# Making the first pairs' sums and stages between the last filter groups, and loading x and v ahead of the spectra

## The chip, the core and the metric

The kernel runs on one core of one Trainium2 chip. The metric is the time of one execution on the device in microseconds. The engines are TensorE (PE, with its weight loads as PEld), VectorE (DVE), ScalarE (ACT), GpSimd (POOL) and SyncE (SP), whose queue issues almost all DMAs. Each engine works through its own instructions in the order in which the program issues them.

## The reference

A long convolution is followed by two MLP blocks. With x and v of shape (2, 12480, 128):

```python
h_filt = (np.maximum(pos_emb @ w1, 0.0) @ w2) * np.exp(-0.01 * pos)[:, None]
u = x * v
L = 2 * S
Uf = np.fft.rfft(u, n=L, axis=1)
Hf = np.fft.rfft(h_filt, n=L, axis=0)
y = np.fft.irfft(Uf * Hf[None], n=L, axis=1)[:, :S, :]
x = (x * y).reshape(B * S, D)
h = x @ moe_w_in;  x = (h * np.cos(h)) @ moe_w_out
h = x @ moe2_w_in; out = (h * np.clip(h + 3.0, 0.0, 6.0) / 6.0) @ moe2_w_out
```

## The kernel before

The order of all instructions is the order of the program (`manual_schedule`). The Fourier transforms are two-stage products with constant matrices, N1 = 111 by N2 = 113. The kernel has three parts.

**The filter** (`hctx`). After the filter's MLP, 16 "turns" add and subtract halves into small buffers `fs` (three of them, taken in rotation; turn 14's sums are GpSimd's, all others VectorE's) and put them through the first stage (`af`), which ScalarE copies to `at`. Then 28 "groups" follow, two at a time: `transform(j)` makes the second stage in PSUM (`fp`) and ScalarE copies it to `ft`; `combine(j)` multiplies with w2 into `pm`, which ScalarE and VectorE copy to `h_a`, `h_b` and `far`. The first 32 channel pairs' spectra (`h_a`, `h_b`) stay on chip. The others, `far`, are written to `spec` in two halves by `send(z)`, 3.1 MB each, on SyncE's queue, once the 14 groups of each half are done.

**The pair loop**, over 64 pairs of channels. For pair i: x and v are loaded (`load`, SyncE); `make_u` multiplies them and then by signs (two GpSimd instructions, `u`); `make_p` copies half of u to PSUM (ScalarE) and `make_f` folds it into `uf[i % 2]` (two VectorE instructions); this is the "sums of a pair" in the change's words. `s1(i, g)`, g = 0 and 1, is the first stage (`ap`, copied to `at`); `s2u(i)` the second stage (`xp`); `mk_pq` and `mk_y` multiply with the spectrum (VectorE, `pq`, `xp` in place in PSUM, `y`); `s2i` and `s1i` are the two inverse stages (`bp`, `v`); `mk_w`, `fin` and `store` end the pair. An iteration i issues work of several pairs: `make_u`, `make_p` and `make_f` of pair i + 2, `s1` of i + 1, `s2u`, `mk_pq`, `mk_y` of i, `s2i` and `s1i` of i - 2, `mk_w` and `fin` of i - 3. Beside it a generator (`decoder`) advances one step per iteration and turns 64-bit weights into two float32r parts. Its first two steps do nothing, its third issues the fetch of the first weights block (`wst`, `wsm`), its fourth issues the first decode instruction (`wd`) on VectorE.

**The MoE phase** is the two MLP blocks, tile by tile of 512 tokens.

What orders the change-over between filter and loop: tiles come from pools. A pool that is opened where closed pools lay can't be written before those closed pools are given back as a whole, that is, before all instructions and DMAs that use their tiles have ended. `ps_d`, `ps_x`, `ps_c`, `ps_p` and `ps_v` (PSUM) lie over `ps_f` and `ps_m` of the groups; `p_d` (buffers of the weights fetch) and `p_w` (`w`, `z`) lie over the pool of `far`; `p_2` (`y`, `b` and, before, `at`) and `p_1` lie over that of the filter's `at` and over `ft`. SyncE issues in program order: load 2, the first spectra write, load 3, the second spectra write, load 4, load 5, the first weights fetch, load 6, and so on.

Of the kernel before, what the change touches and what calls it, by code (L numbers as in the profile page):

```python
# [9 lines left out]
FP32 = mybir.dt.float32  # L10
# [13 lines left out]
N1, N2 = 111, 113  # L24
# [28 lines left out]
def kernel(  # L53
# [115 lines left out]
    def conv_phase(cctx):  # L169
# [35 lines left out]

        ps_a = cctx.enter_context(tc.tile_pool(name="ps_a", bufs=2, space=PSUM))

# [31 lines left out]
        def s1(i, g, pool=None):  # L239
            if i >= NG:  # L240
                return
            if i not in a_t:
                a_t[i] = p_2.tile([KE, 2, 8, K1], FP32, tag="at", name="at")
            at = a_t[i]
            ap = (pool or ps_a).tile([KE, 4, 2, K1], FP32, tag="a", name="ap")
            for q in range(4):
                st = uf[i % 2][:, g, q // 2, q % 2, :KE]
                mm(ap[:, q].rearrange("p z k -> p (z k)"), st, f1[:, :2 * K1], f1[:, K1:])
            nc.scalar.copy(at[:, :, 4 * g:4 * g + 4, :], ap.rearrange("p q z k -> p z q k"))

        with ExitStack() as hctx:
# [12 lines left out]
            with ExitStack() as lctx:  # L264
# [5 lines left out]
                fs = [hp.tile([N1, FG, 128], FP32, name=f"fs{k}") for k in range(3)]  # L270
                ws = hp.tile([N1, MP], FP32, name="ws")
                idle = hp.tile([128, 320], FP32, name="idle")
                nc.vector.memset(idle, 0.0)
# [8 lines left out]
                for t in fs:  # L282
                    nc.gpsimd.memset(t, 0.0)
# [58 lines left out]
                for j, (z, g) in enumerate(turns):  # L342
                    h, f = (hw, hm)[z][:, FG * g:FG * g + FG], fs[j % 3]
                    eng = nc.gpsimd if j == len(turns) - 2 else nc.vector
                    for o, op in ((0, ALU.add), (OD, ALU.subtract)):
                        eng.tensor_tensor(out=f[:, :, o:o + M2], in0=h[:, :, :M2], in1=h[:, :, M2:], op=op)
                    for i in range(2):
                        ap = (ps_a, ps_s)[i].tile([KE, 2, K1, FG // 2], FP32, tag="a", name="af")
                        for q in range(FG // 2):
                            mm(ap[:, :, :, q].rearrange("p z k -> p (z k)"), f[:, FG // 2 * i + q, :KE], f1[:, :2 * K1], f1[:, K1:])  # L350
                        o = R * z + FG * g + FG // 2 * i
                        for y in range(2):
                            nc.scalar.copy(at_z[y][:, :, o:o + FG // 2], ap[:, y])

            with ExitStack() as bctx:
                hf_p = bctx.enter_context(tc.tile_pool(name="hf_p", bufs=3))
                ps_f = bctx.enter_context(tc.tile_pool(name="ps_f", bufs=2, space=PSUM))
                ps_m = bctx.enter_context(tc.tile_pool(name="ps_m", bufs=2, space=PSUM))
# [5 lines left out]
                def transform(j):  # L364
                    if j >= len(groups):
                        return
                    z, k0 = groups[j]
                    fp = ps_f.tile([128, KG, NA2], FP32, tag="f", name="fp")
                    for k in range(KG):
                        mm(fp[:, k, :N2], at_z[z][:, k0 + k], cs[:, z, :N2])  # L370
                    ft[j] = hf_p.tile([128, KG, NA2], FP32, tag="f", name="ft")
                    nc.scalar.copy(ft[j][:, :, :N2], fp[:, :, :N2])
# [20 lines left out]

                transform(0)
                transform(1)
                for j in range(0, len(groups), 2):
                    transform(j + 2)
                    transform(j + 3)
                    combine(j)
                    combine(j + 1)  # L400
                    if groups[j + 1][1] + KG == K1:
                        if groups[j][0]:
                            load(3)
                        send(groups[j][0])
                    if j in (12, 20):
                        make_u(j // 8 - 1)
                    if j in (14, 22):
                        make_p(j // 8 - 1, ps_a)
                        make_f(j // 8 - 1)
# [5 lines left out]
        p_1 = cctx.enter_context(tc.tile_pool(name="p_1", bufs=1))  # L415
        ps_d = cctx.enter_context(tc.tile_pool(name="ps_d", bufs=1, space=PSUM))
        lane = decoder(p_d, ps_d)
        ps_x = cctx.enter_context(tc.tile_pool(name="ps_x", bufs=1, space=PSUM))
        ps_c = cctx.enter_context(tc.tile_pool(name="ps_c", bufs=1, space=PSUM))
        ps_p = cctx.enter_context(tc.tile_pool(name="ps_p", bufs=1, space=PSUM))  # L420
        ps_v = cctx.enter_context(tc.tile_pool(name="ps_v", bufs=1, space=PSUM))

        def s2_mm(o, q0, q1, a):
            for z in range(2):
                mm(o[z], cs[:, z, :N2], a[:, z, q0:q1, :])

        def spectrum(i, z):
            if i >= KA:
                return h_t[i][:, z]
            t, d = (h_a, CH * i) if i < NA else (h_b, CH * (i - NA))  # L430
            return t[:, z, d:d + CH].rearrange("p c s k -> p (c s k)")

        def s2u(i):
            xp = ps_x.tile([N2, 2, 512], FP32, tag="xp", name="xp")
            s2_mm((xp[:, 0, :448], xp[:, 1, :448]), 0, 8, a_t.pop(i))
            xp_t[i] = xp


        def mk_pq(i, b=None):
            if i not in pq_t:  # L440
                xv = xp_t.pop(i)[:, :, :448].rearrange("p z (b k) -> p z b k", b=B)
                pq_t[i] = (p_1.tile([N2, 2, B, 4 * K1], FP32, tag="pq", name="pq"), xv)
            p, xv = pq_t[i]
            for z, o in ((0, p), (1, xv)):
                if b is None:
                    h = spectrum(i, z).unsqueeze(1).unsqueeze(1).to_broadcast([N2, 2, B, 4 * K1])
                    nc.vector.tensor_tensor(out=o, in0=xv, in1=h, op=ALU.mult)
                else:
                    h = spectrum(i, z).unsqueeze(1).to_broadcast([N2, 2, 4 * K1])
                    nc.vector.tensor_tensor(out=o[:, :, b], in0=xv[:, :, b], in1=h, op=ALU.mult)  # L450

        def mk_y(i, b=None):
            p, q = pq_t[i]
            if i not in y_t:
                y_t[i] = p_2.tile([N2, 8, 2 * K1], FP32, tag="y", name="y")
            bs = slice(0, B) if b is None else slice(b, b + 1)
            y = y_t[i][:, 4 * bs.start:4 * bs.stop]
            for z, op in ((0, ALU.subtract), (1, ALU.add)):
                nc.vector.tensor_tensor(
                    out=y[:, :, z * K1:(z + 1) * K1],  # L460
                    in0=p[:, z, bs].rearrange("p b (s k) -> p (b s) k", k=K1),
                    in1=q[:, 1 - z, bs].rearrange("p b (s k) -> p (b s) k", k=K1), op=op,
                )
# [69 lines left out]
        s1(0, 0, ps_c)  # L533
        s1(0, 1)
        for i in range(NG):
            if i:
                load(i + 3)
            load_h(i + 2)
            store(i - 4)
            make_u(i + 2)  # L540
# [14 lines left out]
            if i >= 2:  # L555
                s1i(i - 2)
# [389 lines left out]
```

## Time and profile before

| | |
|---|---|
| median of 3 runs | 2598.14 us (2597.35 to 2599.98) |
| profiled execution | 2598.82 us, of which the span of the profile is 2596.9 |
| filter | up to about 105 us of the span |
| pair loop and its tail | about 107 to 515 us |
| MoE phase | from about 515 us to the end |
| busy over the span | PE 99%, PEld 82%, DVE 90%, ACT 82%, POOL 89% |

A timeline row has the start in us from the start of the span, the length, the engine, the line of the kernel, the operation, the tiles (written <- read), the shapes, and the count of instructions merged into it. What stands in brackets is the idle time of the engine before it and what ended it. Lengths of instructions that follow each other overlap a little, so the difference of two starts is the better price.

### The profile page before, as it was taken

The numbers are of one execution on the slowest core, as the hardware profiler recorded it, in microseconds if no ns is written. First come the engines' busy times: TensorE is split into PE (matmuls) and PEld (weight loads), VectorE is DVE, ScalarE is ACT, GpSimd is POOL, SyncE is SP. The second block draws the span as 40 slices with busy tenths as digits, with TensorE's granted clock in tenths as the row PEclk, the third lists the DMA queues.
The fourth block names the chain that finished last, engine by engine and source line by source line (L and its number), as shares of the span: only waits on it lengthen the run. The fifth ranks groups of instructions, "written<-read, shape, count | busy, mean of one in ns | idle before, by whom it ended". The sixth has DMA issues, their size and how long they took to land.

```text
span 2596.9 us, 45583 instructions
## 1 busy us (share of the span) xinstructions
PE 2566.2 (99%) x16460; PEld 2128.3 (82%) x16460; DVE 2329.5 (90%) x3084; ACT 2121.6 (82%) x3088; POOL 2310.6 (89%) x1206
## 2 busy tenths in 40 slices
PE   8999999989999999999999999999999999999999
PEld 7766666678888888888888888888888888888888
DVE  5599999889999999999999999999999999999997
ACT  5466656589888888888888888888888888888885
POOL 3199999889999999999999999999999999999998
PEclk9999999999999999999999999999999999999999
DMA  2545666400000000000000000000000000000000
GB/s 81 150 131 148 164 170 186 112 17 8 17 12 14 17 9 17 9 17 9 17 9 17 9 17 9 17 16 10 17 9 17 9 17 9 17 9 17 8 9 12
DMA packets 104132, 101.16 MB, mean 39 GB/s; under 512 B 57780, under 2 KB 92774, under 8 KB 103910
## 3 DMA queue, kind: packets, MB, share of 16 engines
q1 hardware_dynamic: 103516, 98.09, 13.9%
q8 instruction: 132, 2.16, 0.4%
q14 instruction: 90, 0.74, 0.1%
q10 hardware_dynamic: 394, 0.17, 0.0%
HBM read 66.00 MB, written 32.22 MB: 38 GB/s over the span
## 4 chain that ended last, share of the span: by engine, by line
PE 79%; ACT 1%; POOL 0%; DVE 0%; issue 0%; DMA 0%; DVEq 0%; ACTq 0%
PE acc L773 39%; PE hb L704 20%; PE ha L704 19%; POOL lo L738 0%; ACT r L725 0%; ACT k L715 0%; DVE g L726 0%; ACT hi L733 0%; DVE r L716 0%; POOL hi L737 0%; POOL z L519 0%; DMA scr<-z 0%; PE xp L235 0%; POOL z L520 0%; POOL z L521 0%
## 5 line engine op out<-in xcount | busy, mean ns | idle before, releaser
L763 POOL TENSOR_TENSOR lo<-g,hi 128x1024 fp32r<-128x1024 f32 (+1 forms) x390 | 938.1, 2406 | 143.0 <-DVE hi L760 133.7
L738 POOL TENSOR_TENSOR lo<-g,hi 128x1024 fp32r<-128x1024 f32 (+1 forms) x392 | 941.3, 2402 | 2.4 <-ACT hi L733 1.8
L773 PE MATMUL acc<-hi,w 128*128 128x512 f32 (+1 forms) x3136 | 813.4, 379 | 0.0
L773 PEld LDWEIGHTS acc<-hi,w 128*128 128x128 f32 x3136 | 589.2, 188 | 99.0
L715 ACT ACTIVATE k<-ha,biasq 128x512 int32<-128x512 f32 (+1 forms) x768 | 494.0, 686 | 212.7 <-PE ha L704 207.2
L726 DVE TENSOR_TENSOR g<-ha,r 128x512 f32<-128x512 f32 (+1 forms) x768 | 499.7, 690 | 171.7 <-ACT r L725 171.7
L704 PE MATMUL hb<-x2h,w 128*128 128x512 f32 (+1 forms) x1564 | 530.5, 379 | 0.0
L725 ACT ACTIVATE r<-r,biaspi 128x512 f32<-128x512 f32 (+1 forms) x776 | 520.5, 719 | 10.4 <-DVE r L716 7.5
L704 PE MATMUL ha<-xh,w 128*128 128x512 f32 (+1 forms) x1524 | 519.1, 381 | 3.2 <-DVE g L726 3.2
L716 DVE SCALAR_TENSOR_TENSOR r<-k,ha 128x512 f32<-128x512 int32 (+1 forms) x768 | 490.2, 681 | 2.6 <-ACT k L715 2.3
L746 DVE SCALAR_TENSOR_TENSOR g<-q,hb 128x1024 f32<-128x1024 f32 (+1 forms) x391 | 473.3, 1210 | 7.1 <-ACT q L745 5.6
L773 PE MATMUL acc<-lo,w 128*128 128x512 f32 (+1 forms) x1568 | 470.1, 380 | 1.0 <-POOL lo L738 1.0
L760 DVE SCALAR_TENSOR_TENSOR hi<-q,hb 128x1024 fp32r<-128x1024 f32 (+1 forms) x390 | 470.4, 1206 | 0.0
L745 ACT ACTIVATE q<-hb,bias 128x1024 f32<-128x1024 f32 (+1 forms) x391 | 429.7, 1099 | 17.9 <-PE hb L704 17.8
L733 ACT CAST hi<-g 128x1024 fp32r<-128x1024 f32 (+1 forms) x385 | 399.6, 1038 | 0.0
L773 PEld LDWEIGHTS acc<-lo,w 128*128 128x128 f32 x1568 | 294.1, 188 | 52.0 <-POOL lo L738 2.7
L704 PEld LDWEIGHTS hb<-x2h,w 128*128 128x128 f32 x1564 | 293.5, 188 | 50.1 <-issue 0.8
L704 PEld LDWEIGHTS ha<-xh,w 128*128 128x128 f32 x1524 | 286.2, 188 | 56.5 <-issue 3.7
L704 PE MATMUL hb<-x2l,w 128*128 128x512 f32 (+1 forms) x782 | 296.5, 379 | 0.0
L704 PE MATMUL ha<-xl,w 128*128 128x512 f32 (+1 forms) x762 | 289.8, 380 | 0.0
L704 PEld LDWEIGHTS hb<-x2l,w 128*128 128x128 f32 x782 | 146.8, 188 | 24.8 <-DVE x2l L783 0.3
L704 PEld LDWEIGHTS ha<-xl,w 128*128 128x128 f32 x762 | 143.2, 188 | 22.6
(145 smaller groups left out, 3201.0 us busy)
## 6 DMA issues: line engine op xcount, KB each, us to landing
x<-in_x_dram SPq DMA_DIRECT2D x64, 199.5 KB
v<-in_v_dram SPq DMA_DIRECT2D x64, 199.5 KB
scr<-z SPq DMA_DIRECT2D x128, 98.9 KB
out_dram<-o SPq DMA_DIRECT2D x47, 256.0 KB
spec<-far SPq DMA_DIRECT2D x2, 3136.0 KB
h<-spec SPq DMA_DIRECT2D x32, 196.0 KB
xf<-scr SPq DMA_DIRECT2D x17, 256.0 KB
wst<-in_wi_dram SPq DMA_DIRECT2D x8, 512.0 KB
```

What stands on the lines that cost most here:

```text
L704: nc.tensor.matmul(out=given(hs[c][:, 0, :n]), lhsT=w["i", e][:, sl], rhs=taken(r[:, :n]), start=(k == 0), stop=(k == 2),)
L715: nc.scalar.activation(out=k[:, c, :n], in_=h, func=ACTF.Identity, bias=biasq, scale=1.0 / TWO_PI)
L716: nc.vector.scalar_tensor_tensor(out=un.r[:, c, :n], in0=k[:, c, :n], scalar=-TWO_PI, in1=h, op0=ALU.mult, op1=ALU.add)
L725: nc.scalar.activation(out=rc, in_=rc, func=ACTF.Sin, bias=biaspi, scale=1.0)
L726: nc.vector.tensor_tensor(out=un.g[:, c, :n], in0=h, in1=rc, op=ALU.mult)
L733: nc.scalar.copy(un.hi[:, :, :n], un.g[:, :, :n])
L738: nc.gpsimd.tensor_tensor(out=un.lo[:, :, :n], in0=un.g[:, :, :n], in1=un.hi[:, :, :n], op=ALU.subtract)
L745: nc.scalar.activation(out=un.r[:, c, :n], in_=h, func=ACTF.Relu, bias=bias3, scale=1.0)
L746: nc.vector.scalar_tensor_tensor(out=un.g[:, c, :n], in0=un.r[:, c, :n], scalar=6.0, in1=h, op0=ALU.min, op1=ALU.mult)
L760: nc.vector.scalar_tensor_tensor(out=un.hi[:, c, :n], in0=un.r[:, c, :n], scalar=6.0, in1=h, op0=ALU.min, op1=ALU.mult)
L763: nc.gpsimd.tensor_tensor(out=un.lo[:, :, :n], in0=un.g[:, :, :n], in1=un.hi[:, :, :n], op=ALU.subtract)
L773: nc.tensor.matmul(out=given(acc[e][:, :n]), lhsT=w["o", e][:, sl], rhs=taken(r[:, c, :n]), start=(u == 0 and c == 0 and k == 0), stop=(u ...
```

## The change

It does six things.

- The filter's buffers `fs` are two instead of three, and `idle`, which feeds matmuls at the start, is the beginning of `fs[1]`, cleared by VectorE.
- `at` of the pair loop and `pq` come from a pool `p_at` that is opened before the filter.
- The groups' `fp` is one tile `fb` of two banks, from `ps_x`, which is opened there; `fp(j)` takes bank j % 2. The loop's `xp` reuses this pool.
- Between the groups stand: loads 3 and 4 ahead of the first spectra write, load 5 ahead of the second; u of pairs 0 to 5; folds of pairs 0 to 3 (`fold`); first stages of pairs 0 and 1; the second stage and one product of pair 0.
- Behind the groups, before `ps_m` is given back: the second stage of pair 1 (in a tile of `ps_m`), the first stage of pair 2, products and y of pairs 0 and 1.
- The loop starts at i = 2, after two decoder steps, and leaves out what has been issued.

`s2_mm`, `spectrum`, `s2u`, `mk_pq` and `mk_y` move up; `mk_pq` takes a choice of halves `zs`, `s2u` a pool and a tag.

```diff
+        p_at = cctx.enter_context(tc.tile_pool(name="p_at", bufs=2))
...
-                a_t[i] = p_2.tile([KE, 2, 8, K1], FP32, tag="at", name="at")
+                a_t[i] = p_at.tile([KE, 2, 8, K1], FP32, tag="at", name="at")
...
+        def s2u(i, pool=None, tag="xp"):
+            xp = (pool or ps_x).tile([N2, 2, 512], FP32, tag=tag, name="xp")
...
+        def mk_pq(i, b=None, zs=range(2)):
...
+                pq_t[i] = (p_at.tile([N2, 2, B, 4 * K1], FP32, tag="pq", name="pq", bufs=1), xv)
...
+        mid = ExitStack()
...
-                fs = [hp.tile([N1, FG, 128], FP32, name=f"fs{k}") for k in range(3)]
+                fs = [hp.tile([N1, FG, 128], FP32, name=f"fs{k}") for k in range(2)]
...
-                idle = hp.tile([128, 320], FP32, name="idle")
-                nc.vector.memset(idle, 0.0)
+                nc.vector.memset(fs[1], 0.0)
+                idle = fs[1].rearrange("p f n -> p (f n)")[:, :320]
...
-                    h, f = (hw, hm)[z][:, FG * g:FG * g + FG], fs[j % 3]
+                    h, f = (hw, hm)[z][:, FG * g:FG * g + FG], fs[j % 2]
...
-                ps_f = bctx.enter_context(tc.tile_pool(name="ps_f", bufs=2, space=PSUM))
-                ps_m = bctx.enter_context(tc.tile_pool(name="ps_m", bufs=2, space=PSUM))
+                ps_x = cctx.enter_context(tc.tile_pool(name="ps_x", bufs=1, space=PSUM))
+                ps_m = mid.enter_context(tc.tile_pool(name="ps_m", bufs=2, space=PSUM))
+                fb = ps_x.tile([128, 2, 512], FP32, tag="xp", name="fb")
...
-                    fp = ps_f.tile([128, KG, NA2], FP32, tag="f", name="fp")
+                    fp = fb[:, j % 2, :KG * NA2].rearrange("p (k n) -> p k n", n=NA2)
...
+                def fold(i):
+                    make_p(i, ps_a)
+                    make_f(i)
+
+                make_u(0)
+                make_u(1)
                 transform(0)
                 transform(1)
                 for j in range(0, len(groups), 2):
...
-                    if groups[j + 1][1] + KG == K1:
-                        if groups[j][0]:
-                            load(3)
-                        send(groups[j][0])
-                    if j in (12, 20):
-                        make_u(j // 8 - 1)
-                    if j in (14, 22):
-                        make_p(j // 8 - 1, ps_a)
-                        make_f(j // 8 - 1)
+                    if j == 12:
+                        load(3)
+                        load(4)
+                        send(0)
+                        fold(0)
+                        make_u(2)
+                    if j == 14:
+                        s1(0, 0)
+                        s1(0, 1)
+                    if j == 16:
+                        fold(1)
+                        make_u(3)
+                        load(5)
+                    if j == 20:
+                        s1(1, 0)
+                        s1(1, 1)
+                        fold(2)
+                        make_u(4)
+                    if j == 24:
+                        s2u(0)
+                        fold(3)
+                        make_u(5)
+                        mk_pq(0, None, (0,))
+                send(1)
...
+        s2u(1, ps_m, "m")
+        s1(2, 0)
+        s1(2, 1)
+        mk_pq(0, None, (1,))
+        mk_y(0)
+        mk_pq(1)
+        mk_y(1)
+        mid.close()
...
-        s1(0, 0, ps_c)
-        s1(0, 1)
-        for i in range(NG):
-            if i:
+        for _ in range(2):
+            step_decode()
+        for i in range(2, NG):
+            if i > 2:
                 load(i + 3)
             load_h(i + 2)
             store(i - 4)
-            make_u(i + 2)
+            if i > 3:
+                make_u(i + 2)
```

## Rows read from the trace of the kernel before

**Rows 1.** Windows view, a steady stretch; columns: PE, PEld, DVE, ACT, POOL, clock, DMA, GB/s.
```profile
200.00:220.00 20.00, 20.00 (x270) 14.01 (x268) 19.22 (x30) 12.45 (x24) 18.59 (x18) 1.00 0.53 131
```

**Rows 2.** Timeline of TensorE, one iteration of the pair loop.
```profile
135.24 0.54 PE L236 MATMUL xp<-at,cs 121*49 121x448 f32 x1
...
136.75 0.55 PE L236 MATMUL v<-b,gm 112*48 112x456 f32 x1
...
138.28 0.26 PE L236 MATMUL bp<-f,y 113*48 113x114 f32 x1
...
141.38 0.54 PE L236 MATMUL xp<-at,cs 121*49 121x448 f32 x1
```

**Rows 3.** Timeline of TensorE, from the last groups to pair 3.
```profile
96.68 2.00 PE L381 MATMUL pm<-w2s,ft 64*113 64x128 f32 x32
...
100.32 2.00 PE L381 MATMUL pm<-w2s,ft 64*113 64x128 f32 x32
103.55 2.03 PE L381 MATMUL pm<-w2s,ft 64*113 64x128 f32 x32 [1.23 <-DVE far L387]
107.18 0.28 PE L235 MATMUL ap<-f,uf 111*64 111x112 f32 x1 [1.60 <-DVE far L387]
...
129.06 0.59 PE L235 MATMUL xp<-at,cs 121*64 121x448 f32 x1 [0.67 <-DVE y L459]
```

**Rows 4.** Timeline of VectorE, groups 24 and 25 and the first iterations.
```profile
102.42 0.39 DVE L386 COPY h_b<-pm 113x224 f32<-113x224 f32 x1 [0.67 <-ACT h_a L385]
...
103.62 0.68 DVE L387 COPY far<-pm 113x512 f32<-113x512 f32 x1
...
124.64 1.17 DVE L231 TENSOR_TENSOR uf<-p,u 111x456 f32<-111x456 f32 x2 [3.45 <-ACT p L223]
125.73 1.08 DVE L447 TENSOR_TENSOR pq<-xp,h_a 113x896 f32<-113x896 f32 x1
...
127.85 1.15 DVE L459 TENSOR_TENSOR y<-pq,xp 113x448 f32<-113x448 f32 x2
128.92 1.17 DVE L490 TENSOR_TENSOR w<-v,v2s 112x456 f32<-112x456 f32 x2
130.00 0.69 DVE L141 TENSOR_SCALAR wd<-wst 128x512 int32<-128x512 int32 x1
```

**Rows 5.** Timeline of SyncE's queue (issues of DMAs), from the second spectra write.
```profile
107.06 7.76 SPq L392 DMA_DIRECT2D spec<-far  x2
...
116.94 1.06 SPq L198 DMA_DIRECT2D v<-in_v_dram  x1
...
120.62 0.35 SPq L111 DMA_DIRECT2D wst<-in_wi_dram  x1
...
121.48 0.43 SPq L197 DMA_DIRECT2D x<-in_x_dram  x1
```

**Rows 6.** Waits of SyncE's queue, 0 to 170: total, times, longest.
```profile
SPq L111 <- DMA spec<-far: 1.0, 1, 1.0
```

**Rows 7.** Timeline of VectorE, the start and the last turns.
```profile
7.44 0.28 DVE L299 TENSOR_TENSOR ws<-win,sig 111x114 f32<-111x114 f32 x1 [6.24 <-DMA sig<-in_sig_dram]
...
45.13 1.18 DVE L346 TENSOR_TENSOR fs<-hm 111x456 f32<-111x456 f32 x2 [0.35 <-PE af L235]
48.19 2.62 DVE L346 TENSOR_TENSOR fs<-hm 111x456 f32<-111x456 f32 x2 [1.89 <-PE af L235]
```

**Rows 8.** Timeline of GpSimd, turn 14 and products of pairs 4 and 6.
```profile
46.86 1.96 POOL L346 TENSOR_TENSOR fs<-hm 111x456 f32<-111x456 f32 x2 [24.75 <-PE af L236]
...
121.64 1.16 POOL L214 TENSOR_TENSOR u<-x,v 112x456 f32<-112x456 f32 x1 [17.38 <-ACT at L249]
...
133.56 1.16 POOL L214 TENSOR_TENSOR u<-x,v 112x456 f32<-112x456 f32 x1
```

**Rows 9.** Groups by line, 0 to 520: busy us, mean ns, idle before.
```profile
L249 ACT COPY at<-ap 121x448 f32<-121x448 f32 x128 | 68.1, 532 | 33.2 <-PE ap L236 33.2
```

**Rows 10.** Windows view, a stretch of the second spectra write, columns as above.
```profile
108.00:111.00 3.00, 3.00 (x56) 2.57 (x54) 0.00 (x0) 1.96 (x4) 0.00 (x0) 1.00 1.01 306
```

More of the change, by code (lines that the diff above doesn't have):

```diff
@@ L249, in s1, with s2_mm, spectrum, mk_y @@
             nc.scalar.copy(at[:, :, 4 * g:4 * g + 4, :], ap.rearrange("p q z k -> p z q k"))
+        def s2_mm(o, q0, q1, a):
+            for z in range(2):
+                mm(o[z], cs[:, z, :N2], a[:, z, q0:q1, :])
+        def spectrum(i, z):
+            if i >= KA:
+                return h_t[i][:, z]
+            t, d = (h_a, CH * i) if i < NA else (h_b, CH * (i - NA))
+            return t[:, z, d:d + CH].rearrange("p c s k -> p (c s k)")
+        def s2u(i, pool=None, tag="xp"):
+            xp = (pool or ps_x).tile([N2, 2, 512], FP32, tag=tag, name="xp")
+            s2_mm((xp[:, 0, :448], xp[:, 1, :448]), 0, 8, a_t.pop(i))
+            xp_t[i] = xp
+        def mk_pq(i, b=None, zs=range(2)):
+            if i not in pq_t:
+                xv = xp_t.pop(i)[:, :, :448].rearrange("p z (b k) -> p z b k", b=B)
+                pq_t[i] = (p_at.tile([N2, 2, B, 4 * K1], FP32, tag="pq", name="pq", bufs=1), xv)
+            p, xv = pq_t[i]
+            for z in zs:
+                o = (p, xv)[z]
+                if b is None:
+                    h = spectrum(i, z).unsqueeze(1).unsqueeze(1).to_broadcast([N2, 2, B, 4 * K1])
+                    nc.vector.tensor_tensor(out=o, in0=xv, in1=h, op=ALU.mult)
+                else:
+                    h = spectrum(i, z).unsqueeze(1).to_broadcast([N2, 2, 4 * K1])
+                    nc.vector.tensor_tensor(out=o[:, :, b], in0=xv[:, :, b], in1=h, op=ALU.mult)
+        def mk_y(i, b=None):
+            p, q = pq_t[i]
+            if i not in y_t:
+                y_t[i] = p_2.tile([N2, 8, 2 * K1], FP32, tag="y", name="y")
+            bs = slice(0, B) if b is None else slice(b, b + 1)
+            y = y_t[i][:, 4 * bs.start:4 * bs.stop]
+            for z, op in ((0, ALU.subtract), (1, ALU.add)):
+                nc.vector.tensor_tensor(
+                    out=y[:, :, z * K1:(z + 1) * K1],
+                    in0=p[:, z, bs].rearrange("p b (s k) -> p (b s) k", k=K1),
+                    in1=q[:, 1 - z, bs].rearrange("p b (s k) -> p (b s) k", k=K1), op=op,
+                )
+        mid = ExitStack()
         with ExitStack() as hctx:
@@ L281, in conv_phase @@
                     nc.tensor.matmul(out=busy, lhsT=idle[:, :128], rhs=idle)
-                for t in fs:
-                    nc.gpsimd.memset(t, 0.0)
+                nc.gpsimd.memset(fs[0], 0.0)
                 def load_pos(k):
@@ L415, in conv_phase @@
         p_1 = cctx.enter_context(tc.tile_pool(name="p_1", bufs=1))
+        s2u(1, ps_m, "m")
[6 more added lines that the diff above has]
+        mid.close()
         ps_d = cctx.enter_context(tc.tile_pool(name="ps_d", bufs=1, space=PSUM))
         lane = decoder(p_d, ps_d)
-        ps_x = cctx.enter_context(tc.tile_pool(name="ps_x", bufs=1, space=PSUM))
+        ps_v = cctx.enter_context(tc.tile_pool(name="ps_v", bufs=1, space=PSUM))
@@ L419, in conv_phase @@
         ps_c = cctx.enter_context(tc.tile_pool(name="ps_c", bufs=1, space=PSUM))
         ps_p = cctx.enter_context(tc.tile_pool(name="ps_p", bufs=1, space=PSUM))
[L421 to L463, printed above, removed]
@@ L554, in conv_phase @@
                 break
-            if i >= 2:
-                s1i(i - 2)
+            s1i(i - 2)
             mk_pq(i)
```

## The prediction

> **What bounds the kernel now.** I read the windows view first. In a steady stretch of the pair loop TensorE is busy for the whole of it, VectorE for 19.2 of 20 us and GpSimd for 18.6, at full granted clock [rows 1]. TensorE's timeline of one iteration says which of them sets the pace [rows 2]: the second stage `xp` starts at 135.24, the inverse first stage `v` at 136.75 (1.51 us), the four half-pair sets `bp`, `ap`, `bp`, `ap` fill 138.28 to 141.38 (0.78 apiece), and then the next `xp`: 6.14 us, and no row of the four has a wait in brackets. VectorE's own work in an iteration is 5.4 us [rows 4] and 0.6 more for each decode instruction, so it is close behind. What the loop gains must therefore come out of TensorE idle time, and that lies in one place, the change-over [rows 3]: from the matmuls of filter groups 24 and 25 (100.32, which end near 102.3) to `xp` of pair 3 (129.06) pass 26.8 us. Work in them: groups 26 and 27 1.95, five first stages at 1.55, three second stages at 1.51, two `bp` pairs at 1.55, one `v` at 1.53, together 18.9. So some 7.9 us of idle time is all that this change can take on TensorE. After 129.06 the loop, the tail and the MoE phase follow without slack on TensorE, so a shift there reaches the end one for one.
>
> VectorE in the same stretch [rows 4]: folds of pair 4 at 124.64 after 3.45 us of waiting, then one block without a gap: the two products (`pq` and `xp`) 2.12, `y` 1.07, `w` 1.08, and at 130.00 the first decode instruction `wd`. From 124.64 no row of VectorE has a wait, so 130.00 is the mark against which I measure. SyncE's queue [rows 5]: the second spectra write is issued at 107.06, x and v of pair 4 behind it, and the first weights block `wst` at 120.62. The view of waits says what that fetch waited for: the spectra write itself [rows 6].
>
> **The change part by part.** *Two filter buffers for three.* A turn takes 1.53 us (two turns lie between 45.13 and 48.19), and VectorE fills a buffer in 1.18, so two buffers carry the ordinary turns with some 0.2 us to spare [rows 7]. Turn 14 is GpSimd's: 1.96 us from 46.86, when turn 11 is freed [rows 8]. With two buffers it has to wait for turn 12: 48.39 to 50.35, where turn 13 ends on TensorE near 49.7: 0.7 us lost. VectorE's turn 15 starts at 49.72 beside GpSimd and takes the 2.62 us of its row, to 52.34, where TensorE would be free at 51.9: 0.5 more. I take 1.2 us, between 0.7 (if turn 15 takes only 1.18) and 1.8 (if the 0.6 us in which the two overlap doubles for GpSimd too). On the cause of the 2.62 the Trainium skill (SBUF — State Buffer, "Who interferes with whom") says that a VectorE instruction with two SBUF inputs contends with a GpSimd instruction that reads SBUF, and that the later one blocks until the first ends. The row agrees, 2.62 against 1.18; taken as strict turns with GpSimd's 1.16 us sums the rule would give about 1.6 us in place of 1.2, and the forecast would be 0.4 us later. The longer clearing of `fs[1]` (for `idle`) goes into 6.24 us in which VectorE waits for the signs' load until 7.44 [rows 7]; without that cover it would be under a microsecond.
>
> *Folds, first stages and loads moved between the groups.* Two groups take TensorE 3.64 us (96.68 to 100.32 [rows 3]). `s1` of pairs 0 and 1 adds 4 x 0.78 = 3.1, which is moved work, not new work. On VectorE the copies of two groups run from 102.42 to 104.30, 1.9 us of 3.63 [rows 4], so one fold (1.1) fits behind them, and there is one at j = 12, 16, 20 and 24 each. On ScalarE a copy of `at` costs 0.53 [rows 9]; three of them behind the groups' own copies delay at most one `ft` by 0.3 us, which TensorE doesn't need for another microsecond. GpSimd's products for pairs 2 to 5 are eight sums of 1.16 us [rows 8], 9 us in over 50, and each pair's u is ready one pair of groups or more before its fold. Loads 3 and 4 go out ahead of the first spectra write and load 5 behind it, before the second. So SyncE, which had loads 4 and 5 (four DMAs) behind the second write, now has only the fetch of `wst` and `wsm` and then load 6 there. `make_u(4)` had started at 121.64, when v of pair 4 (issued 116.94) had come [rows 5, 8]: that wait goes. `pq` in `p_at`, `fb` as two banks of one tile and the moved definitions issue the same instructions; I cost them at nothing, with `fb` as a rival below.
>
> *The end of the groups.* TensorE ends group 25 at 102.3 + 3.1 + 1.2 = 106.6. `s2u(0)` follows (1.5) and then groups 26 and 27, to 110.1, without the old wait of 1.23. VectorE: copies of 24 and 25 to 108.6, folds of pair 3 to 109.7, first half of `pq` to 110.7, copies of groups 26 and 27 to 112.6. So the second spectra are complete at 112.6, where it was 107.06: 5.5 us later. Then `pq`'s other half, `y(0)`, both halves of `pq(1)` and `y(1)`: 1.1 + 1.1 + 2.1 + 1.1, to 118.0.
>
> *The new wait.* `s1(3, 0, ps_c)` takes a bank that lay in `ps_m`, and the pool as a whole has to be given back first; before, the first stage at 107.18 likewise waited 1.60 for the last copy of group 27, whose tile isn't in its bank [rows 3]. Now the last reader of `ps_m` is `y(1)`, so TensorE stands from about 115.7 (behind `s1(2)` and `s2i(0, 0)`) to 118.1. Queued behind it: `s2i(0, 1)`, `s1(3, 1)`, `s2u(2)`, and through ScalarE's order the copy `p(4)`, for which VectorE's folds of pair 4 wait. Three sets (2.3) and ScalarE's last two copies with their hand-overs (1.3): the folds start at 121.7, 2.9 us ahead of 124.64. `xp` of pair 3 comes at 118.1 + 2.3 + 1.5 + 1.5 + 3.1 = 126.5, 2.5 ahead of 129.06. Up to here the change gains 2.5 us, the rest of the 7.9 being left in about 1.6 us before `s2u(1)` (a bank of group 26), 2.4 at this wait and the 1.2 of the buffers.
>
> *What is late next.* VectorE reaches `w(0)` at 126.0 and `wd` at 127.1. `wd` needs `wst`, whose buffer lies where `far` lay, so the fetch waits until the spectra write has been read out [rows 6], and that starts 5.5 us later. Before, issue at 107.06 to the fetch at 120.62 took 13.5 us. From below: 3.14 MB at the 306 GB/s of its stretch [rows 10] and 0.9 from issue to the first bytes, 11.2. Its tail had load 4 beside it, which is gone, so I take 12.8: the fetch goes out at 125.4. Its landing isn't shown. From below 0.9 + 0.52 MB at 306 GB/s, 2.6 us; from above 9.4, since `wd` at 130.00 didn't wait. The nearest row is v of pair 4, issued 116.94 and used at 121.64: 4.7, which I take. So `wd` at 130.1 against 130.00, with VectorE idle for some 3 us before it; folds of pair 5, `pq(3)` and `y(3)` follow at the old times, and TensorE, which came 2.5 us early, waits for them. The same write must be out before `w(0)`, whose pool also lies over `far`; at 125.4 against 126.0 that just passes. The second gate says the same as the first: load 6 is issued 0.9 behind the fetch, with 1.46 MB ahead of its end, and lands near 133, where `make_u(6)` ran at 133.56 [rows 8]. The sum: 2598.82 (profiled execution) + 0.1, and by the same shift 2598.14 + 0.1 for the median, 2598.2. The Trainium skill (DMA: Bandwidth & Descriptors, "Anatomy of one DMA — SWDGE (gpsimd) path") prices a DMA at about 2.0 us and its bytes at 436 GB/s, fitted on GpSimd's queue: by that the fetch lands in 3.2 us and the whole would be 1.4 us lower. No row here shows a weights fetch's landing.
>
> **The rivals.** *The gate opens early.* With 11.2 for the write and 2.6 for the fetch, `wst` is there at 126.4 and nothing holds VectorE; the gain is TensorE's 2.5: 2595.6. For it: load 4 is gone from the tail. Against: 306 GB/s comes at a DMA share of 1.01 [rows 10], and every row has more than the bytes alone. *Slower: the first weights block comes late.* One mechanism: VectorE stands at `wd`, in order, with `w(1)`, the folds of pair 5 and `pq(3)` behind it. It decides once the fetch takes over 4.6 us from 125.4; each microsecond more costs about one, as TensorE then waits for `y`. At the upper bound, 9.4, `wd` comes at 134.8: 2602.9. Against: the old 9.4 had load 5 ahead of it. *`fb` couples the transforms.* If the two banks of one tile were ordered as one, each of 26 transforms would wait for the copy before it (0.53 [rows 9] and about 0.15 of hand-over): 18 us, 2616. Against: `pt` is loaded and read slice by slice in one tile already. *The change does all it can.* Neither the pool nor the fetch holds: 7.9 less the buffers' 1.2 gives 6.7, 2591.4. Against: [rows 3, 6] show both waits.
>
> **How the numbers follow.** Forecast (gate near 130, 2596.7 to 2599.7) 0.56; early gate 0.26; late block 0.10; coupled transforms 0.03; full gain 0.05. The prediction is 2598.2. 0.2% is 5.2 us, about what a measurement of this kernel can tell from no change. The range runs from 2595.2 (just under the early gate's 2595.6) to 2601.0, a little past the middle of the late block, and leaves out the two last cases and half of the late one, 0.13. Faster by over 0.2% is the full gain alone, 0.05; slower by as much the coupled transforms and the corner where the latest block meets the buffers' upper bound (2602.9 + 0.6), 0.05; the rest 0.90.
>
> **What would show it.** In the changed profile: turn 15's sums near 49.7 and TensorE's pause before turns 14 and 15; the second spectra write issued near 112.6; a TensorE wait of over 2 us for `y` before an `ap` near 118; folds of pair 4 near 121.7; the first `wst` fetch near 125.4, and VectorE idle about 3 us before the first `wd` near 130. I'm wrong if `wd` starts without a wait (then 2.5 us faster), if the transforms show idle time between them, or if the spectra are complete before 110.

## The result, and the profile after

| | before | after |
|---|---|---|
| median (4 runs each) | 2599.06 us (2597.35 to 2601.40) | 2613.76 us (2613.04 to 2614.19) |
| span of the profiled execution | 2596.9 us | 2611.2 us |

The ratio is 1.0054 (95% interval 1.0043 to 1.0066): slower by some 14 us, where 2598.2 was predicted with a range up to 2601.0. The loss is all there before the loop runs evenly. The second stage `xp` of pair 3 starts at 142.03, where it was 129.06 [rows 3], 13.0 us later, and that of pair 8 at 174.69 against 159.99, 14.7 later. From there to the last pair both kernels take the same, 340.7 and 340.9 us.

TensorE's waits in the changed kernel between 45 and 130 us (engine, line and tile, what it waited for; us in total, times, longest) show where.

```profile
PE fb L235 <- ACT ft L416: 10.3, 15, 0.8
PE xp L235 <- DVE far L431: 1.5, 1, 1.5
PE af L236 <- POOL fs L389: 0.5, 1, 0.5
...
PE af L236 <- DVE fs L389: 0.2, 1, 0.2
```

The first row has no counterpart before. TensorE's timeline of one pair of groups shows one of these fifteen waits:

```profile
78.91 2.01 PE L425 MATMUL pm<-w2s,ft 64*113 64x128 f32 x32
80.84 0.31 PE L235 MATMUL fb<-cs,at 121*64 121x113 f32 x1
...
82.53 0.31 PE L235 MATMUL fb<-cs,at 121*64 121x113 f32 x1 [0.70 <-ACT ft L416]
...
83.46 2.00 PE L425 MATMUL pm<-w2s,ft 64*113 64x128 f32 x32
```

and ScalarE's of the same stretch what it waited for:

```profile
81.94 0.54 ACT L416 COPY ft<-fb 128x452 f32<-128x452 f32 x1 [0.58 <-PE fb L236]
```

The second transform of the pair writes the other bank of `fb`, yet it starts only once ScalarE has copied the first one's (81.94 to 82.48). From `pm` to `pm` a pair of groups takes 4.55 us (78.91 to 83.46), where it took 3.64 [rows 3]: 0.70 of waiting, and 0.2 more that stand in no row of waits. The likely reason is that TensorE's pipeline runs empty and fills again (a matmul takes 0.26 by itself, while in sequence one starts every 0.10).

Behind the groups the changed kernel does what was forecast, some 14 us late. SyncE's queue:

```profile
126.22 7.96 SPq L436 DMA_DIRECT2D spec<-far  x2
139.29 0.35 SPq L111 DMA_DIRECT2D wst<-in_wi_dram  x1
```

VectorE, folds of pair 4 and the first decode instruction:

```profile
136.34 1.17 DVE L231 TENSOR_TENSOR uf<-p,u 111x456 f32<-111x456 f32 x2 [4.56 <-ACT p L223]
...
143.94 0.69 DVE L141 TENSOR_SCALAR wd<-wst 128x512 int32<-128x512 int32 x1 [1.98 <-DMA wst<-in_wi_dram]
```

They answer to [rows 5] (107.06, 120.62) and [rows 4] (124.64, 130.00): the write 19.2 us later, the fetch 18.7, the first decode 13.9, and now it waits.

### The profile page after: what moved, and what is told of

It reads as the page before. It is cut to its first block, busy times and chain, and to the rows that moved or that the text cites. A ratio compares the mean times of both kernels' runs of the same rounds, so it can differ in the third digit from the quotient of the medians.

```text
span 2611.2 us, 45581 instructions
## 1 busy us (share of the span) xinstructions
PE 2572.3 (99%) x16460; PEld 2130.9 (82%) x16460; DVE 2329.2 (89%) x3084; ACT 2121.1 (81%) x3088; POOL 2311.9 (89%) x1204
## 4 chain that ended last, share of the span: by engine, by line
PE 78%; ACT 1%; DVE 0%; POOL 0%; DMA 0%; issue 0%; SPq 0%; ACTq 0%; DVEq 0%
PE acc L803 39%; PE hb L734 20%; PE ha L734 19%; POOL lo L768 0%; ACT k L745 0%; ACT r L755 0%; DMA x<-z 0%; DVE g L756 0%; ACT hi L763 0%; DVE r L746 0%; SPq L617 0%; POOL hi L767 0%; PE xp L235 0%; DVE w L543 0%; DVE pq L279 0%
## 5 line engine op out<-in xcount | busy, mean ns | idle before, releaser
L734 PEld LDWEIGHTS hb<-x2h,w 128*128 128x128 f32 x1564 | 293.5, 188 | 50.1 <-issue 0.8
```

What stands on the lines that cost most here:

```text
L734: nc.tensor.matmul(out=given(hs[c][:, 0, :n]), lhsT=w["i", e][:, sl], rhs=taken(r[:, :n]), start=(k == 0), stop=(k == 2),)
```

## The experiments

"Coupling" is the theory that the two banks of `fb`, as one tile, are ordered as one. Its first rival is that the work moved between the groups costs the time. No kernel leaves out any work. "Marks" are times in the profiled execution, one for each kernel. With two filter buffers turn 3's sums start between 29.6 and 32.1 in executions whose edits change nothing ahead of them, so single microseconds are read from distances between marks and from waits, not from absolute marks or medians alone.

**1. Two tiles in the changed kernel** (`e1_two_tiles`)

```diff
-                ps_x = cctx.enter_context(tc.tile_pool(name="ps_x", bufs=1, space=PSUM))
...
-                fb = ps_x.tile([128, 2, 512], FP32, tag="xp", name="fb")
...
+                ps_f = fctx.enter_context(tc.tile_pool(name="ps_f", bufs=2, space=PSUM))
+                ps_m = mid.enter_context(tc.tile_pool(name="ps_m", bufs=2, space=PSUM, side="right"))
...
-                    fp = fb[:, j % 2, :KG * NA2].rearrange("p (k n) -> p k n", n=NA2)
+                    fp = ps_f.tile([128, KG, NA2], FP32, tag="f", name="fp")
...
                     if j == 24:
+                        fctx.close()
+                        ps_x = cctx.enter_context(tc.tile_pool(name="ps_x", bufs=1, space=PSUM))
                         s2u(0)
```

> The changed kernel with the groups' second stage in two tiles of one bank each, as before the change, instead of two banks of one tile. Theory 'coupling': the one tile makes each transform wait for ScalarE's copy of the one before; that is 0.91 us for each of 13 pairs of groups (4.55 against 3.64) and 2.0 at the first four transforms, 13.8 in all, so 2613.8 - 13.8 = 2600.0, with what is left as forecast: 2598 to 2600.5, no idle time before a transform, the second spectra write issued near 112.6. Theory 'moved work': the folds, first stages and copies put between the groups hold TensorE up; then the idle time stays and the time is 2610 or more.

Measured: 2599.89 us, ratio to before 1.0007 (0.9998 to 1.0016); span 2598.0, 13.2 under the changed kernel's. The fifteen waits are gone and none of the moved work was taken back, so what is left of the change costs no more than the interval allows and the coupling is the loss. This kernel is also the change as the prediction meant it, so the steps can be judged in it. TensorE around the wait for the pool:

```profile
117.89 0.31 PE L235 MATMUL ap<-f,uf 111*64 111x112 f32 x1 [2.29 <-DVE y L288]
...
118.71 0.35 PE L235 MATMUL bp<-f,y 113*64 113x114 f32 x1
...
120.18 0.39 PE L235 MATMUL ap<-f,uf 111*64 111x112 f32 x1
...
121.68 0.79 PE L235 MATMUL xp<-at,cs 121*64 121x448 f32 x1
...
128.08 0.54 PE L235 MATMUL xp<-at,cs 121*64 121x448 f32 x1
```

Windows of the same place (columns as in [rows 1]; the clock is the third number from the end):

```profile
117.90:118.70 0.80, 0.80 (x16) 0.80 (x18) 0.00 (x0) 0.00 (x0) 0.00 (x0) 1.00 1.02 323
118.70:121.70 3.00, 3.00 (x38) 3.00 (x36) 0.00 (x0) 1.08 (x2) 0.00 (x0) 0.51 1.04 326
```

SyncE and VectorE:

```profile
112.28 7.86 SPq L436 DMA_DIRECT2D spec<-far  x2
125.34 0.35 SPq L111 DMA_DIRECT2D wst<-in_wi_dram  x1
```

```profile
122.95 1.17 DVE L231 TENSOR_TENSOR uf<-p,u 111x456 f32<-111x456 f32 x2 [5.12 <-ACT p L223]
130.32 0.79 DVE L141 TENSOR_SCALAR wd<-wst 128x512 int32<-128x512 int32 x1 [1.92 <-DMA wst<-in_wi_dram]
137.71 1.17 DVE L231 TENSOR_TENSOR uf<-p,u 111x456 f32<-111x456 f32 x2 [0.66 <-ACT p L223]
```

ScalarE's copies behind the last turns, and GpSimd's product of pair 6:

```profile
49.72 0.59 ACT L396 COPY at<-af 121x224 f32<-121x224 f32 x2 [0.17 <-PE af L236]
51.23 0.59 ACT L396 COPY at<-af 121x224 f32<-121x224 f32 x2 [0.91 <-PE af L236]
51.99 0.59 ACT L396 COPY at<-af 121x224 f32<-121x224 f32 x2 [0.17 <-PE af L236]
53.22 0.59 ACT L396 COPY at<-af 121x224 f32<-121x224 f32 x2 [0.63 <-PE af L236]
```

```profile
134.69 1.16 POOL L214 TENSOR_TENSOR u<-x,v 112x456 f32<-112x456 f32 x1 [2.77 <-ACT at L249]
```

**2. One tile in the kernel before** (`e2_one_tile_before`)

```diff
-                ps_f = bctx.enter_context(tc.tile_pool(name="ps_f", bufs=2, space=PSUM))
+                ps_f = bctx.enter_context(tc.tile_pool(name="ps_f", bufs=1, space=PSUM))
+                fb = ps_f.tile([128, 2, 512], FP32, tag="f", name="fb")
...
-                    fp = ps_f.tile([128, KG, NA2], FP32, tag="f", name="fp")
+                    fp = fb[:, j % 2, :KG * NA2].rearrange("p (k n) -> p k n", n=NA2)
```

> The kernel before, with nothing changed but the groups' second stage in two banks of one tile. 'Coupling': everything behind comes 13.8 us later, 2599.1 + 13.8 = 2612.9 (2611.5 to 2614). 'Moved work': no difference, 2598 to 2600.

Measured: 2611.99 us, ratio 1.0051 (1.0039 to 1.0064), span 2610.1, 13.2 over before's. The view of TensorE's waits has the same row as the changed kernel:

```profile
PE fb L235 <- ACT ft L373: 10.3, 15, 0.7
```

One edit, put in or taken out, moves the span by the same 13.2 us in both kernels. From the first transform to the end of the last combine it moves the groups by 13.5 in both (52.99 to 66.47 here, 56.38 to 69.85 with the moved work), so the start of an execution has no part in it.

**3. One tile, a combine between the two transforms** (`e7_between`)

```diff
                     transform(j + 2)
-                    transform(j + 3)
                     combine(j)
+                    transform(j + 3)
                     combine(j + 1)
```

> The changed kernel, still with one tile of two banks, but the order in a pair of groups is transform, combine, transform, combine instead of two transforms and two combines, so that ScalarE's copy of a bank (0.54 us and its hand-over) lies beside a combine (0.97). 'Coupling' as an order of one tile's accesses: the wait is covered and the time is that of the run with two tiles, 2599.9 (2598.5 to 2601). If instead the two banks themselves or ScalarE's load hold TensorE, the idle time stays: 2611 or more.

Measured: 2605.71 us, ratio 1.0027 (1.0017 to 1.0037), between the two. The waits within the pairs are gone; only two of the first transforms, which follow each other without a combine, still wait (1.3 us in all). But TensorE's timeline shows a new price (the window cuts the last row short):

```profile
78.56 1.13 PE L425 MATMUL pm<-w2s,ft 64*113 64x128 f32 x16
79.62 0.31 PE L235 MATMUL fb<-cs,at 121*64 121x113 f32 x1
...
80.55 1.13 PE L425 MATMUL pm<-w2s,ft 64*113 64x128 f32 x16
...
82.53 0.70 PE L425 MATMUL pm<-w2s,ft 64*113 64x128 f32 x8
```

From 78.56 to 82.53 a pair takes 3.97, 0.33 more than in one piece: TensorE changes between the two kinds of matmul four times instead of twice, which comes to some 0.17 for each more. Over the 13 pairs that hold both kinds that is 4.3 us; with the 1.3 it makes the 5.6 by which the second spectra write comes later than with two tiles (117.91 against 112.28). The time forecast for coupling alone (2598.5 to 2601) was missed by this price; that the waits go when only the order changes speaks for coupling all the same, and against the moved work.

**4. The loads alone, in the kernel before** (`e5_loads_before`): loads 3 and 4 ahead of the first spectra write (load 3 had stood ahead of the second), load 5 and u of pair 2 ahead of the second; nothing else.

```diff
                         if groups[j][0]:
+                            make_u(2)
+                            load(5)
+                        else:
                             load(3)
+                            load(4)
                         send(groups[j][0])
...
```

> The kernel before, with loads 3 and 4 ahead of the first spectra write and load 5 (with the products of pair 2, which free its buffer) ahead of the second; no stage moved. Theory 'queue': in the kernel before, the folds of pair 4 wait 3.45 us because load 4 lies behind the spectra write; they then start 2.5 us earlier and the fetch of the first weights comes early enough: 2596.6 (2596 to 2597.5). Rival 'hidden': another wait (the spectra write before the weights' fetch) takes its place: 2598.5 to 2599.5.

Measured: 2597.07 us, ratio 0.9994 (0.9985 to 1.0003). The interval includes no change at all. Pair 8 comes at 158.73, 1.26 ahead of before (1.7 counted from turn 3's sums). VectorE's rows bear the queue out: folds of pair 4 wait 0.83 where it was 3.45 [rows 4], and the first decode comes 2.1 earlier, without a wait. So load 4 it was that u of pair 4 had waited for, although [rows 8] name ScalarE's copy `at`, which `make_u` doesn't read.

```profile
122.53 1.17 DVE L231 TENSOR_TENSOR uf<-p,u 111x456 f32<-111x456 f32 x2 [0.83 <-ACT p L223]
...
127.89 0.70 DVE L141 TENSOR_SCALAR wd<-wst 128x512 int32<-128x512 int32 x1
```

**5. Without TensorE's wait for the pool** (`e8_pool_split`, on two tiles): `ps_m` is two pools of one buffer, and the one that `s1` of pair 3 needs is given back ahead of `mk_y`.

```diff
-                ps_m = mid.enter_context(tc.tile_pool(name="ps_m", bufs=2, space=PSUM, side="right"))
+                ps_m = [mid.enter_context(tc.tile_pool(name="ps_m0", bufs=1, space=PSUM, side="right")),
+                        mid1.enter_context(tc.tile_pool(name="ps_m1", bufs=1, space=PSUM, side="right"))]
...
+        mid1.close()
+        ps_c = cctx.enter_context(tc.tile_pool(name="ps_c", bufs=1, space=PSUM))
```

> The run with two tiles, with the pool of the combines' tiles split in two, so that the first stage of pair 3 doesn't wait for y of pair 1. Theory 'fetch': the first decode instruction still starts near 130, since the weights' fetch waits for the spectra write; TensorE reaches the second stage of pair 3 some 3 us earlier and gives it back before pair 8; 2599.9 within 0.6. Theory 'pool': the wait for the pool is what costs, and the time falls by 2.3 to 3.5: 2596.5 to 2597.6.

Measured: 2600.96 us, ratio 1.0018 (0.9996 to 1.0040; one execution of eleven, at 2631.06, pulls it up, and the medians alone give 1.0010), span 2597.9 against 2598.0 with the wait. That is half a microsecond above what 'fetch' allowed and far from what 'pool' promised. `xp` of pair 3 comes at 123.75, 5.3 us ahead of before, and pair 8 at 160.76, where it was 159.99. VectorE's rows say where the 5.3 went:

```profile
125.22 1.17 DVE L525 TENSOR_TENSOR w<-v,v2s 112x456 f32<-112x456 f32 x2 [2.00 <-DMA spec<-far]
129.59 0.69 DVE L141 TENSOR_SCALAR wd<-wst 128x512 int32<-128x512 int32 x1 [3.20 <-DMA wst<-in_wi_dram]
```

`w` waits for the spectra write and `wd` for the fetch. TensorE then waits 3.99 us for ScalarE, where the copy `v2s`, out of the PSUM bank that `ap` needs, stands in order behind the decoder's first ScalarE instructions, and those behind `wd`:

```profile
130.32 0.66 ACT L142 ACTIVATE wd<-wd,b_exp 128x512 int32<-128x512 int32 x1 [5.36 <-DVE wd L141]
...
131.60 0.54 ACT L519 COPY v2s<-v 112x456 f32<-112x456 f32 x1
```

```profile
132.20 0.45 PE L235 MATMUL ap<-f,uf 111*64 111x112 f32 x1 [3.99 <-ACT v2s L519]
```

**6. The fetch not behind the spectra write's end** (`e4_fetch_free`, on two tiles): `p_d` is opened last, so it doesn't lie over `far`.

```diff
-        p_d = cctx.enter_context(tc.tile_pool(name="p_d", bufs=1))
         p_w = cctx.enter_context(tc.tile_pool(name="p_w", bufs=2))
...
+        gap = p_g.tile([128, 704], FP32, name="gap")
         p_2 = cctx.enter_context(tc.tile_pool(name="p_2", bufs=2))
+        p_s = cctx.enter_context(tc.tile_pool(name="p_s", bufs=1))
+        p_d = cctx.enter_context(tc.tile_pool(name="p_d", bufs=1))
```

> The run with two tiles, with the buffers of the weights' fetch where the second spectra don't lie, so that the fetch doesn't wait for the spectra write; the rest of the layout moves accordingly. 'Fetch': the first decode instruction no longer waits, the 1.0 us that TensorE has gained at pair 3 is kept at pair 8 instead of turning into 1.1 lost: 2.1 us below the run with two tiles, 2597.8. 'Pool': no difference, 2599.9 within 0.5.

Measured: 2597.41 us, ratio 0.9993 (0.9984 to 1.0002). SyncE issues the fetch 8.3 us behind the write instead of 13.1, and `wd` has no wait:

```profile
113.24 8.15 SPq L436 DMA_DIRECT2D spec<-far  x2
121.50 1.83 SPq L111 DMA_DIRECT2D wst<-in_wi_dram  x1
```

From pair 3 to pair 8 it takes 30.93 us, with two tiles alone 33.04: 2.1 us, as expected. So the fetch was the gate, as in [rows 6], and with it load 6, which follows it in the queue: u of pair 6 starts at 132.68 here, with two tiles alone at 134.69.

**7. Turn 14 by VectorE** (`e3_turn14_vector`, on two tiles), and **GpSimd held as well** (`e9_gpsimd_held`, on the free fetch)

```diff
-                    eng = nc.gpsimd if j == len(turns) - 2 else nc.vector
+                    eng = nc.vector
```

and for the second, behind the turns:

```diff
+                nc.gpsimd.tensor_tensor(out=hold, in0=fs[1][:, 0, :1], in1=fs[1][:, 0, :1], op=ALU.mult)
```

> The changed kernel with two tiles, and turn 14's sums by VectorE instead of GpSimd. If the two filter buffers cost what was forecast, and the weights' fetch hangs on the spectra write and so on the end of the filter, it is 1.2 us (0.7 to 1.5) below the run with two tiles alone. If the fetch doesn't set the time, or VectorE becomes late instead, no difference, within 0.4.

> The kernel with two filter tiles and the fetch's buffers away from far, turn 14 by VectorE, and one product of one element on GpSimd behind the turns that reads the last sums, so that GpSimd can't start u of pair 0 before them. Theory 'collision' (turn 14's change gained nothing because GpSimd, no longer held, made u of pairs 0 and 1 beside VectorE's first turns, whose four sums took 4.15 us instead of 2.26): the four sums take 2.3 again, no wait of TensorE for the sums, and pair 8 starts 0.8 us earlier from turn 3 than in the kernel with the fetch free (127.1 instead of 127.9); median 2596 to 2597. Rival 'no collision' (the start varies by itself): the four sums take about 4 us again or pair 8 is no earlier; median 2597.4 or more.

The first took 2599.54 us, ratio 1.0005 (0.9996 to 1.0013). The waits for the sums of turns 14 and 15 (0.5 and 0.2 in the changed kernel) are gone, but no gain came. VectorE's first four sums (with its folds of pair 4 for later) and GpSimd's rows beside them say why:

```profile
24.24 4.15 DVE L389 TENSOR_TENSOR fs<-hw 111x456 f32<-111x456 f32 x4
...
121.95 1.18 DVE L231 TENSOR_TENSOR uf<-p,u 111x456 f32<-111x456 f32 x2 [3.65 <-ACT p L223]
```

```profile
23.06 1.15 POOL L216 TENSOR_TENSOR u<-u,sig 112x456 f32<-112x456 f32 x1
24.17 1.15 POOL L214 TENSOR_TENSOR u<-x,v 112x456 f32<-112x456 f32 x1
25.39 1.42 POOL L216 TENSOR_TENSOR u<-u,sig 112x456 f32<-112x456 f32 x1
```

Turn 14 had kept GpSimd, which works in order, from u of pairs 0 and 1 until it was done (at 50.1 with two tiles). Without it GpSimd made them at once, beside the sums that TensorE was waiting for: 4.15 us for four. The change won its 1.2 us at the other end: from TensorE's first matmul of turn 13 to the first transform it takes 4.51 us, with two tiles alone 5.72. But from turn 0 to turn 3 it takes 8.35 instead of 6.95. With GpSimd held until the last sums the four take 2.26 again:

```profile
23.59 2.26 DVE L390 TENSOR_TENSOR fs<-hw 111x456 f32<-111x456 f32 x4
```

Measured there: 2597.17 us, ratio 0.9988 (0.9979 to 0.9997); pair 8 is 125.2 behind turn 3's sums, where it was 127.9 with the free fetch. The collision is shown by the sums. Of the 2.7 only 0.8 was expected; 1.2 lie at turns 14 and 15 (5.72 and 4.52 from turn 13 to the first transform), and most of the rest is TensorE's clock, which stayed up here after its wait of 2.29 and fell in the kernel with the free fetch (below). The profiled execution, at 2593.0, is the fastest of eleven: four took up to 2594.5, the other seven 2596.8 and more. So its marks aren't those of the median, and of the time itself 0.9988 against 0.9993 shows no difference.

**8. All waits taken away** (`e6_all`: turn 14 by VectorE, the pool split, `p_d` and `p_w` clear of `far`, load 6 ahead of the second spectra write), **with GpSimd held** (`e10_all_held`), and **the first fetch ahead of the second spectra write** (`e11_fetch_first`). The edit of the last:

```diff
-                send(1)
+            z1ctx.close()
+            p_d = cctx.enter_context(tc.tile_pool(name="p_d", bufs=1, side="right"))
+            first = fetch_high(order[0], p_d), fetch_mid(order[0], p_d)
+            send(1)
```

> Two tiles, turn 14 by VectorE, the combines' pool split, the weights' fetch and w where the second spectra don't lie, and load 6 ahead of the second spectra write. If the waits named are all of what the change leaves on the path, TensorE reaches the second stage of pair 3 near 124 and keeps 4 to 5 us: 2594 (2592.5 to 2595.5), below both kernels. If yet another wait takes their place, 2597 to 2599.

> The kernel with all waits removed that were known, and GpSimd held as in the run above. Theory 'collision': the four sums take 2.3 instead of 4.17, everything behind comes 1.5 to 1.9 us earlier, pair 8 at 157.5 to 158, median about 2596. The fetch still stands behind the spectra write, so VectorE still waits 3 to 3.5 us at the first decode instruction. Rival: pair 8 at 159.4 and 2597.7 as without the hold.

> As the run above, with the first weights fetch issued ahead of the second spectra write, into buffers where the at of the filter's second half lay. Theory 'fetch is the gate': the fetch goes out near 110, VectorE doesn't wait for it, TensorE's wait of 2.6 us before the first stage of pair 4 goes, pair 8 starts near 155, median 2593 to 2594, which beats the kernel before by about 4.5 us. Rival 'another wait takes its place once more' (the spectra write before w, or GpSimd's products): pair 8 not before 157, median 2595.5 or more.

Measured: 2597.71 us, ratio 0.9998 (0.9989 to 1.0007); with the hold 2596.61, 0.9988 (0.9979 to 0.9997), pair 8 at 158.98, hardly earlier than without it (159.35) and 1 us later than expected; with the fetch first 2596.11, 0.9988 (0.9979 to 0.9997), pair 8 at 155.02. The four sums take 2.3 again with the hold, but from turn 0 to turn 3 TensorE takes 7.65, where it was 8.08 without the hold and 6.75 in `e9_gpsimd_held`: its granted clock is 0.50 from 25.0 to 31.6 here, and there from 25.4 to 28.6 only. In `e6_all` no tile stands in the fetch's way, but SyncE issues it behind the spectra write, and it is used 7.2 us later:

```profile
112.56 8.28 SPq L438 DMA_DIRECT2D spec<-far  x2
120.95 1.99 SPq L111 DMA_DIRECT2D wst<-in_wi_dram  x1
```

```profile
128.13 0.69 DVE L141 TENSOR_SCALAR wd<-wst 128x512 int32<-128x512 int32 x1 [3.41 <-DMA wst<-in_wi_dram]
```

So the queue itself was the next gate. With the fetch ahead of the write that gate is open too, and TensorE's wait of 2.57 before `ap`, which ends at 130.73 in `e6_all`, shrinks to 0.2:

```profile
108.46 0.35 SPq L111 DMA_DIRECT2D wst<-in_wi_dram  x1
110.68 8.83 SPq L441 DMA_DIRECT2D spec<-far  x2
```

```profile
122.75 0.68 DVE L141 TENSOR_SCALAR wd<-wst 128x512 int32<-128x512 int32 x1
```

By the mark the expected 155 came true, but 1.4 of the 4.0 us by which it is ahead of the kernel with the hold lie in the start (turn 3's sums at 30.74 and 32.14), and its clock stays at 1.00 from 110 to 150 where the other's falls to 0.50 behind its wait of 2.55. The median gained 3.2 us on before (0.8 to 5.5), somewhat less than the 4.5 expected but with them inside the interval. This version and the two others of 0.9988 beat both kernels, before by some 0.1%, with intervals that end just under 1.

## Why the prediction was wrong

**The step that failed** is the sentence "`pq` in `p_at`, `fb` as two banks of one tile and the moved definitions issue the same instructions; I cost them at nothing". They do issue the same instructions, but not with the same waits. As one tile, TensorE's write to one bank waits for ScalarE's read of the other: 13.2 us, shown by putting the edit in and taking it out. It was the rival of the coupled transforms that came true, at a chance of 0.03. What spoke against it is true of `pt` (TensorE reads its first slices at 3.69, while the last load is issued at 5.7), but it is another case: there a read waits for the load of its own slice, here a write comes behind a read of the other part. Why the one is ordered by slices and the other by the tile stays open.

**The size of that rival** was 18 us, with a wait for each of 26 transforms. Only the second transform of a pair waits: the first one's copy ends under the two combines. The first four transforms cost 2.5 (6.63 from the first transform to the first combine, 4.13 with two tiles) and each of the twelve pairs behind them 0.92 (4.55 against 3.63 with two tiles), together the 13.5 of the groups.

**The steps behind it held**, read in the kernel with two tiles: the second spectra write at 112.28 (112.6 forecast); TensorE's wait for `y` 2.29, to 117.89 (2.4, to 118.1); the fetch 13.06 behind the write (12.8), at 125.34 (125.4); `wd` 4.98 behind the fetch (4.7), at 130.32 (130.1). In the changed kernel itself the same two distances are 13.07 and 4.65. For the landing the Trainium skill (DMA: Bandwidth & Descriptors, "Anatomy of one DMA — SWDGE (gpsimd) path") gave an estimate of 3.2; SyncE's queue shows 4.36 to 4.98 in the five kernels that fetch behind the write and wait for it, and the measurement decides. That the gate at `wd` gives back what TensorE gained, and that no gain would be left, was right: ratio 1.0007 with two tiles. Its path was another at first: TensorE was to wait for `y`, and its next wait is for ScalarE's `v2s` (0.93 with two tiles, 3.99 in `e8_pool_split`).

**Mis-sized terms.** Folds of pair 4 came at 122.95 and `xp` of pair 3 at 128.08, 1.3 and 1.6 later than forecast. That is TensorE's clock: after the wait of 2.29 the windows show 0.51 from 118.70 to 121.70, the level of 1.2 GHz, and two half-pair sets took 2.97 (118.71 to 121.68) instead of 1.56. It isn't bound to the edit. With turn 14 on VectorE the same wait of 2.29 stands before the same `ap`, and the windows behind it read

```profile
118.30:119.10 0.80, 0.76 (x16) 0.76 (x18) 0.00 (x0) 0.00 (x0) 0.00 (x0) 1.00 1.00 306
119.10:122.00 2.90, 2.90 (x46) 2.16 (x44) 0.05 (x1) 2.06 (x4) 0.00 (x0) 1.00 1.04 331
```

Full clock, and there the folds come at 121.95 and `xp` of pair 3 at 126.87, 0.3 and 0.4 from the forecast. So the working of this term was right and lacked a clock that may fall; [rows 3] show waits of 1.23 and 1.60 only. The kernel with turn 14 on VectorE met the fall later: its TensorE waits 2.35 for `v2s`, to 133.20, and the granted clock is 0.50 from 134.6 to 137.8.

The second gate was mis-sized too. Load 6 was to land near 133, in time for u of pair 6 at the old 133.56; with two tiles u of pair 6 starts at 134.69, 1.1 later, after GpSimd has waited 2.77. The row names ScalarE's `at`, but what `make_u` needs last is load 6, and the trace has the last update of its DMAs at 134.53. ScalarE's `p` and the folds at 137.71 (0.66 of waiting) come behind it, and pair 8 is 1.1 later than before, where the prediction had 0.1.

**A term that held.** The buffers cost the 1.2 us of the forecast. ScalarE's copies behind the turns, 0.77 apart otherwise, are once 1.51 and once 1.23 apart (49.72 to 51.23, 51.99 to 53.22), 1.2 more in all; from turn 13 to the first transform it takes 5.72 us, before 4.52. TensorE's rows of waits show 0.5 and 0.2 of it only: as with the transforms, a wait costs more than the idle time that is listed.

**The gain's bound** was right in kind: 6.7 us if neither pool nor fetch held, 7.9 without the buffers' 1.2. With pool, fetch and buffers out of the way, `e11_fetch_first` is 5.0 ahead of before at pair 8 (4.4 counted from TensorE's turn 3).

## What to carry to other kernels

Two banks that one engine writes while another reads the other should be two tiles: an edit that only merges them adds waits though every instruction stays the same, and the idle time in front of the first instruction of each use shows it. The listed idle time is not the whole price (0.70 cost 0.91), so take it from the distance of two marks. When a wait at a change-over is taken away, look for the next gate before counting the gain, here the pool, then the fetch's buffer, then the queue in front of the fetch. Before an instruction is moved off an engine that works in order, see what it had held back there.

## What the runs showed that I had not expected

- One and the same wait of TensorE, 2.28 or 2.29 us before `ap`, was followed by a granted clock of 0.5 for some 3 us in three kernels (the changed one, two tiles, the free fetch) and by 1.00 in three others (turn 14 on VectorE, the combine between, GpSimd held). Waits of 1.23 and 1.60 left it at full clock; the later waits for `v2s` of 2.22 (the combine between), 2.35 (turn 14 on VectorE), 2.55, 2.57 and 3.99 were followed by 0.50. So a wait of 2.22 could cost the clock and one of 2.29 spare it: the length of the wait alone doesn't decide, and what does stays open. Where the clock fell it cost about 1.6 us more.
- Each further change between the two kinds of matmul came to some 0.17 us of TensorE (3.97 against 3.64 for a pair of groups).
- SyncE's fetch of a weights block took 4.36 to 4.98 us from issue to use, and 6.9 to 7.2 where it was issued behind a spectra write that was still being moved.
- Four sums on VectorE took 4.15 us beside GpSimd's products and 2.26 without them.
